# The wo products by one Strassen level, in a gated mix of windowed attention and a gMLP

## The chip, the cores and the metric

The kernel runs on 1 core of one Trainium2 chip. The metric is the device time of one execution in microseconds (us), the median of several runs; less is better. A core has TensorE (PE, matmuls into PSUM), VectorE (DVE), ScalarE (ACT), GpSimd (POOL) and SyncE (SP, which issues nearly all DMA here). Each engine takes its instructions in the order in which the program lists them.

## The reference

`x` is 2048 rows of 1024. All inputs are bfloat16.

```python
g = sigmoid((x * gate_w).sum(-1))
# A: 32 heads of 32, each position sees itself and 7 earlier ones, 2 apart
o = attention(x @ wqkv)                       # 2048 x 1024
a = o @ wo                                    # 1024 x 1024
# B: gMLP, half width 1792
z = gelu(x @ w_in); z1 = z[:, :1792]; z2 = layernorm(z[:, 1792:])
b = (z1 * (w_sp @ z2 + b_sp)) @ w_out         # w_sp is 2048 x 2048
out = g * a + (1 - g) * b
```

## The kernel before

One launch goes through stages that keep TensorE busy one after the other: the first z2 columns and the q, k, v projection of eight groups of four heads (L614), the rest of z2 (L319), z1 (L717), the mixer w_sp @ z2 (L732), the wo products (L890), and the gate stage, y @ w_out with the final sum (L732 again). The attention itself runs on VectorE, from the projection into the mixer, and writes o to DRAM in head order (`store_o`, L396).

The mixer and the gate stage already use one Strassen level (Winograd's form): a pair of row tiles of 128 is split in 2 x 2 blocks, and seven products take the place of eight. Operands are float16, scaled by powers of two that are read off the sum of absolute values, so that the sums of blocks do not overflow; an `Abs` activation with `accum_out` gives row sums, a matmul with a matrix of ones adds them over the partitions, and bit operations on the exponent make a power of two. In `g_group(n)` (mixer groups n = 0 to 15, each a pair of tiles and half of the columns) the products go to two PSUM banks `pa` and `pd` and a third bank `pb` that is forked off `pa` by ScalarE after the first product:

```python
product(pa, v.a11, b11, f0, f1, True)
pb = fork(pa, ZC, lo)
product(pd, v.s1, t1, f0, f1, True)
p5 = keep(pd, None)
product(pa, v.s2, t2, f0, f1, False)
u2 = keep(pa, lo)
```

So the third product waits for the fork (L756), the fifth for the snapshot `keep` (L742, L744), the seventh for the next one; `vec` (L748) adds on VectorE, L783 evicts the last product, L784 multiplies with z1. `y_norm` (L570) sums the absolute values of the group, `y_finish` scales it to float16 (L584) and `store_y` (L540) writes it to DRAM. For each pair the rows of w_sp are loaded transposed (`load_rows`, L485), scaled by VectorE (`scale_rows`, L492) and summed (`s_sums`, L496, L497).

The wo products take the o rows back transposed (`load_oT`, L455, 16 tiles of 128 rows into 16 places), with wo in the same order from DRAM (`load_wo`, L450), in bfloat16: 16 tiles x 2 halves of 512 columns x 8 matmuls. ScalarE evicts each half times the gate `g_s` into `mix` (L892). The gate stage adds `mix` at its end.

The order is by hand: `tc.manual_schedule()`, and a class `Beat` that counts the time TensorE ought to take (`BEAT`), and at the end of each product puts into the program what is due: steps given with `beat.at(time, fn)`. It decides order alone; when a step runs is up to the engines' queues. `w_out` is summed in eight pieces in the z1 stage (`load_w_piece` L547, `w_norm` L550), and loaded and scaled late (`load_w_out` L848 to L851, `w_scale` L856, `w_sums` L866, `y_sums` L870).

Of the kernel before, what the change touches and what calls it, by code (L numbers as in the profile page):

```python
# [10 lines left out]
F32 = mybir.dt.float32  # L11
# [4 lines left out]
P = 128  # L16
# [45 lines left out]
def kernel(  # L62
# [25 lines left out]
    def reg(off, n):  # L88
        return arena[:, off:off + n]
# [54 lines left out]
    yl = sm.tile([P, 32], F32, name="yl")  # L144
    ys = sm.tile([P, 16], F32, name="ys")
    wl = sm.tile([P, 8], F32, name="wl")
    wl_n = sm.tile([P, 1], BF, name="wl_n")
    wsc = sm.tile([P, 1], F32, name="wsc")
    rs_n = sm.tile([P, 16], BF, name="rs_n")
    cm05 = sm.tile([P, 16], F32, name="cm05")  # L150
    nc.gpsimd.memset(cm05[:], -0.5)
    att_L = sm.tile([P, 2 * W * 8 * HG], F32, name="att_L")
# [35 lines left out]
    class Pair:  # L188
        def __init__(self, off):
# [11 lines left out]
    snaps = [reg(o, 2 * ZC).bitcast(F32) for o in  # L201
             [X_OFF + 14336, X_OFF + 14336 + 896, SN_OFF, SN_OFF + 896, SN_OFF + 1792]]
    abs_waste = reg(SN_OFF + 2688, 896).rearrange("p (h f) -> p h f", h=2)
    rs_bc = [rs_b[:, 256 * r:256 * (r + 1)] for r in range(2)]

    y_ring = [reg(X_OFF + 7168 + r * 1792, 1792).bitcast(F16).rearrange("p (r h f) -> p r h f", r=2, h=2)
# [7 lines left out]
    e1, e2, e4 = [reg(F_OFF + 3584 * r, 3584).bitcast(F16).rearrange("p (k n) -> p k n", n=512) for r in range(3)]  # L214
    e3 = d12
    w_flat = B_w_out.rearrange("(p a) n -> p (a n)", p=P)
    w_pieces = [reg(T2_OFF + 3584 + 1792 * r, 1792) for r in range(2)]

    class Rows:
        def __init__(self, off):  # L220
# [7 lines left out]
    rows = [Rows(o) for o in (F_OFF + 10752, F_OFF + 17024, A_OFF, A_OFF + 6272, A_OFF + 12544)]  # L228
    keeps = [reg(S0_OFF + 1024 * r, 1024).bitcast(F32) for r in range(7)]
    mix = [reg(o, 2048).bitcast(F32) for o in [Z_OFF + 2048 * r for r in range(14)] + [T1_OFF, T1_OFF + 2048]]  # L230
    oT = [reg(o, 1024).rearrange("p (k t) -> p k t", k=KT)
          for o in [A_OFF + 1024 * r for r in range(11)] + [S0_OFF + 1024 * r for r in range(5)]]
    wo_sb = reg(A_OFF + 11264, KT * D).rearrange("p (k n) -> p k n", k=KT)
    ob_slots = [reg(o, 1024) for o in [F_OFF + 23296, F_OFF + 24320] + [Z_OFF + 2048 * r for r in range(14)]]

    x_v = x2.rearrange("(i q) d -> q i d", q=P)
# [188 lines left out]
    def attended():  # L425
        store_o(NG - 1)
        load_wo()
        prep["attended"] = True

    prep = {"at": 1e12, "normed": 0, "done": False, "attended": False, "o": 0}  # L430

    def vector_steps(t):
        for item in attention_steps(t):
# [13 lines left out]
                           A_wo.rearrange("(g h d) n -> h g d n", g=NG, h=HG, d=DH)[h])  # L447

    def load_wo():
        sync.dma_start(wo_sb, wop_d.rearrange("(k p) n -> p k n", p=P))  # L450

    def load_oT(limit):
        n = prep["o"]
        if n < limit:
            sync.dma_start_transpose(oT[n], o_d[n * P:(n + 1) * P, :])  # L455
            prep["o"] += 1

    def load_nat(a, slot):
        sync.dma_start(slot, wsp_v[a])
# [89 lines left out]
    def w_norm(m):  # L549
        nc.scalar.activation(w_pieces[m % 2], w_pieces[m % 2], ACT.Abs, accum_out=wl[:, m:m + 1])  # L550

    def w_total():
        nc.vector.memset(zeros[:], 1.0)
        nc.vector.tensor_reduce(wsc[:], wl[:], AX.X, ALU.add)
        nc.vector.tensor_copy(wl_n[:], wsc[:])

    def w_power():
        ps = psum.tile([P, 512], F32, name="ps", tag="ps")
        nc.tensor.matmul(ps[:, 0:1], ones, wl_n[:], start=True, stop=True)
        nc.vector.tensor_scalar(wsc[:], ps[:, 0:1], 2.0 ** -30, 2.0 ** -13, ALU.max, ALU.mult)  # L560
        nc.vector.tensor_scalar(wsc[:].bitcast(U32), wsc[:].bitcast(U32), EXPO, EXPO, ALU.bitwise_and, ALU.bitwise_xor)

    def load_rows_y(u):
        for r in range(2):
# [2 lines left out]
    def y_norm(n):  # L567
        for r in range(2):
            k = 2 * (2 * (n // 2) + r) + n % 2
            nc.scalar.activation(abs_waste, g_ring[n % 4][:, r], ACT.Abs, accum_out=yl[:, k:k + 1])  # L570

    def y_power(u):
        sl = slice(2 * u, 2 * u + 2)
# [125 lines left out]
    beat.at(t + 20.0, row_store)  # L699
    beat.at(t + 22.0, lambda: load_scale(0))  # L700
    for m in range(8):
        beat.at(t + 30.0 + 4.2 * m, lambda m=m: load_w_piece(m))
        beat.at(t + 36.5 + 4.2 * m, lambda m=m: w_norm(m))
    beat.at(t + 70.0, w_total)
    beat.at(t + 91.0, w_power)

    for c in range(4):
        w1 = w1_slots[c]
# [16 lines left out]
                                       ap=[[FH, P], [P * FH, 4], [1, ZC]]), z1s)  # L725
    assert prep["done"]
    beat.lead = MIX_LEAD

    def product(ps, w, v, c0, c1, first):
        K = v.shape[1]  # L730
# [82 lines left out]

    for n in range(2):
        load_z1(n)
    for n in range(2 * NU):
        u, fb = n // 2, n % 2
        t = beat.now
        if fb == 0 and u + 1 < NU:
            beat.at(t + 0.5, lambda u=u: load_scale(u + 1))  # L820
            for h in range(2):
                beat.at(t + 2.0, lambda u=u, h=h: load_rows(u + 1, h))
        g_group(n)
        if fb == 0 and u > 0:
            y_finish(u - 1)
        if fb == 0 and u + 1 < NU:
            for h in range(2):
                scale_rows(u + 1, h)
            beat.on_vector(2.5)
            for fn in s_sums(u + 1):  # L830
                fn()
            beat.on_vector(2.8)
        if prep["attended"]:
            limit = 16 if n >= 2 * NU - 3 else 11
            for m in range(6):
                beat.at(beat.now + 1.0 + 1.6 * m, lambda limit=limit: load_oT(limit))
    assert prep["attended"]

    t = beat.now
    beat.at(t + 5.0, lambda: y_norm(2 * NU - 1))  # L840
    beat.at(t + 7.0, lambda: y_finish(NU - 1))
    for m in range(16):
        beat.at(t + 1.0 + 1.6 * m, lambda: load_oT(16))

    def load_w_out(b):
        w = w_out_n[:, 7168 * b:7168 * (b + 1)].rearrange("p (k n) -> p k n", n=D)
# [6 lines left out]
    def w_scale(b):  # L853
        for m in range(4):
            sl = slice(7168 * b + 1792 * m, 7168 * b + 1792 * (m + 1))
            nc.vector.tensor_scalar(w_out_h[:, sl], w_out_n[:, sl], wsc[:], None, ALU.mult)  # L856

    def omegas():
        for x in (ys[:], wsc[:]):
            nc.vector.tensor_scalar(x.bitcast(U32), x.bitcast(U32), EXPO, EXPO, ALU.bitwise_and, ALU.bitwise_xor)  # L860
        nc.vector.scalar_tensor_tensor(omr[:], ys[:], 0.5, omr[:], ALU.mult, ALU.mult)
        nc.vector.tensor_scalar(omr[:], omr[:], wsc[:], 0.5, ALU.mult, ALU.mult)

    def w_sums():
        for out_, a, b in ((e1, d12, d11), (e2, d22, e1), (e3, d22, d12), (e4, d21, e2)):
            TT(out_, a, b, ALU.subtract)  # L866

    def y_sums(u):
        v = rows[u % 5]
# [2 lines left out]
        TT(v.s2, v.s1, v.a11, ALU.subtract)  # L872
        TT(v.s4, v.a12, v.s2, ALU.subtract)

    beat.at(t + 3.0, lambda: load_w_out(0))
    beat.at(t + 20.0, lambda: w_scale(0))
    beat.at(t + 30.0, lambda: w_scale(1))
    beat.at(t + 32.0, w_sums)
    beat.at(t + 36.0, omegas)
    for u in range(2):  # L880
        beat.at(t + 26.0 + 4.0 * u, lambda u=u: load_rows_y(u))
        beat.at(t + 44.0 + 4.0 * u, lambda u=u: y_sums(u))

    for a in range(16):
        if a == 12:
            beat.at(beat.now + 0.5, lambda: load_rows_y(2))
        for c in range(2):
            psa = bank()
            for kt in range(KT):
                nc.tensor.matmul(psa[:], oT[a][:, kt, :], wo_sb[:, kt, 512 * c:512 * (c + 1)],  # L890
                                 start=(kt == 0), stop=(kt == KT - 1))
            nc.scalar.activation(mix[a][:, 512 * c:512 * (c + 1)], psa[:], ACT.Copy, scale=g_s[:, a:a + 1])  # L892
            beat.run(KT * 512)
    beat.flush(1e9)

    kept = [0]
# [4 lines left out]
        nc.scalar.activation(out, ps[:], ACT.Copy, scale=scale)  # L901
        return out

    def finish(out, ps, scale, x):
        nc.vector.scalar_tensor_tensor(out, ps[:], scale, x, ALU.mult, ALU.add)  # L905

    for u in range(NU):
        v = rows[u % 5]
        lo, hi = [omr[:, 2 * u + h:2 * u + h + 1] for h in range(2)]
        m11, m12, m21, m22 = [mix[2 * u + h][:, 512 * c:512 * (c + 1)] for h in range(2) for c in range(2)]  # L910
        o11, o12, o21, o22 = [ob_slots[2 * u + h][:, 512 * c:512 * (c + 1)] for h in range(2) for c in range(2)]
        pa, pd = [psum.tile([P, 512], F32, name="ps", tag="ps") for _ in range(2)]
        if u == 0:
            for n in (3, 4):
                load_rows_y(n)
        product(pa, v.a11, d11, 0, 512, True)
        pb = fork(pa, 512, None)
        product(pd, v.s1, e1, 0, 512, True)
        p5 = hold(pd, hi)
        product(pa, v.s2, e2, 0, 512, False)  # L920
        u2 = hold(pa, lo)
        product(pb, v.a12, d21, 0, 512, False)
        finish(o11, pb, lo, m11)
        TT(u2, u2, m12, ALU.add)
        product(pa, v.s3, e3, 0, 512, False)
        u3 = hold(pa, hi)
        TT(p5, p5, m22, ALU.add)
        if 0 < u < NU - 1:
            y_sums(u + 1)
        product(pd, v.s4, d22, 0, 512, False)  # L930
        TT(o22, p5, u3, ALU.add)
        finish(o12, pd, lo, u2)
        sync.dma_start(out2[2 * u * P:(2 * u + 1) * P, :], ob_slots[2 * u])
        product(pa, v.a22, e4, 0, 512, False)
        finish(o21, pa, hi, m21)
        if u == NU - 1:
            sync.dma_start(out2[(2 * u + 1) * P:(2 * u + 2) * P, 512:D], o22)
            sync.dma_start(out2[(2 * u + 1) * P:(2 * u + 2) * P, 0:512], o21)
        else:
            sync.dma_start(out2[(2 * u + 1) * P:(2 * u + 2) * P, :], ob_slots[2 * u + 1])  # L940
        if u + 5 < NU:
            load_rows_y(u + 5)
# [30 lines left out]
```

## Time and profile before

| | us |
|---|---|
| median of 3 runs (lowest to highest) | 684.23 (683.94 to 684.54) |
| the profiled execution, its own time | 688.53 |
| its span, first to last instruction | 686.8 |
| z1 stage, start to end on TensorE | 270.6 to 369.8 |
| mixer | 369.8 to 543.3 |
| wo stage | 543.3 to 598.5 |
| gate stage | from 598.5 |

The mean granted clock is 0.998. Times in the text are counted from the start of the span. In lines of a timeline the first number is the start, the second the duration (of several instructions together where "x" is over 1), and a bracket is the idle time of the engine before it with what ended it. "SPq" lines are the issue of DMA, with the waiting of the queue.

### The profile page before, as it was taken

The numbers are of one execution on the slowest core, as the hardware profiler recorded it, in microseconds if no ns is written. First come the engines' busy times: TensorE is split into PE (matmuls) and PEld (weight loads), VectorE is DVE, ScalarE is ACT, GpSimd is POOL, SyncE is SP. The second block draws the span as 40 slices with busy tenths as digits, with TensorE's granted clock in tenths as the row PEclk, the third lists the DMA queues.
The fourth block names the chain that finished last, engine by engine and source line by source line (L and its number), as shares of the span: only waits on it lengthen the run. The fifth ranks groups of instructions, "written<-read, shape, count | busy, mean of one in ns | idle before, by whom it ended". The sixth has DMA issues, their size and how long they took to land.

```text
span 686.8 us, 9395 instructions
## 1 busy us (share of the span) xinstructions
PE 676.4 (98%) x3612; PEld 395.3 (58%) x3618; DVE 513.3 (75%) x554; ACT 366.8 (53%) x690; POOL 13.2 (2%) x23
## 2 busy tenths in 40 slices
PE   9999999999999999999899999999998999999997
PEld 4577788888875555555455555555554444444443
DVE  0009799999999999999999999999925356045645
ACT  4345666565545887848863464545544453422221
POOL 1000000000000000012100000000000000000000
PEclk9999999999999999999999999999999999999999
DMA  8999779999759751446845735595489997155211
GB/s 228 174 227 233 213 184 269 252 248 223 202 123 269 272 173 57 166 102 204 295 141 174 151 84 147 137 255 156 135 207 252 246 276 156 26 113 128 72 62 61
DMA packets 229148, 121.80 MB, mean 177 GB/s; under 512 B 190832, under 2 KB 215664, under 8 KB 229104
## 3 DMA queue, kind: packets, MB, share of 16 engines
q1 hardware_dynamic: 229104, 121.21, 67.1%
q8 instruction: 28, 0.46, 0.3%
q14 instruction: 16, 0.13, 0.1%
HBM read 61.87 MB, written 37.82 MB: 145 GB/s over the span
## 4 chain that ended last, share of the span: by engine, by line
PE 92%; DMA 3%; ACT 2%; SPq 2%; issue 0%; DVE 0%; ACTq 0%
PE ps L732 32%; PE ps L614 18%; PE ps L319 9%; PE ps L717 8%; PE sd L614 6%; PE ps L890 6%; PE seed L732 5%; PE sd L319 3%; PE sd L717 3%; PE sd L890 2%; SPq L599 1%; DMA z_d<-arena 1%; DMA arena<-in_A_wqkv_dram 1%; DMA y_d<-arena 1%; ACT arena L719 1%; ACT arena L550 1%
## 5 line engine op out<-in xcount | busy, mean ns | idle before, releaser
L732 PE MATMUL ps<-arena 128*128 128x448 f16 (+1 forms) x1104 | 223.9, 362 | 2.2 <-ACT arena L744 2.2
L732 PEld LDWEIGHTS <-arena 128*128 128x128 f16 x1288 | 126.5, 98 | 131.6 <-issue 4.5
L614 PEld LDWEIGHTS <-arena 128*128 128x128 bf16 x1024 | 141.6, 138 | 26.1 <-issue 1.4
L614 PE MATMUL ps<-arena 128*128 128x384 bf16 x768 | 130.3, 326 | 1.0 <-DMA arena<-in_A_wqkv_dram 1.0
L342 DVE TENSOR_TENSOR arena<-arena 128x8192 bf16<-128x8192 bf16 x16 | 70.8, 4422 | 47.3 <-DMA arena<-in_A_wqkv_dram 47.1
L345 DVE TENSOR_TENSOR arena<-arena 128x4096 bf16<-128x4096 bf16 (+1 forms) x64 | 77.6, 1212 | 2.0
L717 PEld LDWEIGHTS <-arena 128*128 128x128 bf16 x512 | 49.9, 98 | 48.5 <-issue 2.1
L717 PE MATMUL ps<-arena 128*128 128x448 bf16 x384 | 75.6, 352 | 1.8 <-ACT arena L719 1.8
L319 PE MATMUL ps<-arena 128*128 128x448 bf16 (+1 forms) x384 | 76.8, 353 | 0.5 <-DMA arena<-in_B_w_in_dram 0.5
L319 PEld LDWEIGHTS <-arena 128*128 128x128 bf16 x512 | 49.9, 98 | 47.1 <-ACT arena L306 0.7
L375 DVE TENSOR_TENSOR arena<-arena,att_A 128x8192 bf16<-128x8192 bf16 x16 | 70.7, 4421 | 0.2
L622 ACT CAST arena<-ps 128x384 bf16<-128x384 f32 x84 | 39.5, 484 | 45.0 <-PE ps L614 41.9
L905 DVE SCALAR_TENSOR_TENSOR arena<-seed,omr,arena 128x512 bf16<-128x512 f32 x8 | 6.0, 751 | 59.3 <-PE seed L732 59.3
L614 PE MATMUL sd<-arena 128*128 128x384 bf16 x256 | 46.8, 326 | 0.0
L890 PE MATMUL ps<-arena 128*128 128x512 bf16 x187 | 42.3, 379 | 0.2
L890 PEld LDWEIGHTS <-arena 128*128 128x128 bf16 x256 | 25.0, 98 | 30.2
L732 PE MATMUL seed<-arena 128*128 128x448 f16 (+1 forms) x184 | 40.2, 361 | 0.0
L325 ACT ACTIVATE arena<-ps 128x448 bf16<-128x448 f32 x48 | 26.1, 548 | 24.5 <-PE ps L319 23.9
L719 ACT ACTIVATE arena<-ps 128x448 bf16<-128x448 f32 x48 | 25.5, 570 | 25.4 <-PE ps L717 25.3
L381 DVE TENSOR_TENSOR arena<-arena 128x4096 bf16<-128x4096 bf16 x16 | 36.6, 2290 | 0.4
L744 ACT ACTIVATE arena<-ps,bt 128x448 f32<-128x448 f32 x32 | 20.3, 634 | 29.5 <-PE ps L732 29.4
L901 ACT ACTIVATE arena<-ps,omr 128x512 f32<-128x512 f32 x24 | 16.5, 688 | 32.7 <-PE ps L732 32.7
(121 smaller groups left out, 632.1 us busy)
## 6 DMA issues: line engine op xcount, KB each, us to landing
arena<-in_B_w_sp_dram SPq DMA_DIRECT2D x16, 512.0 KB, 5.2
arena<-k_d SPq DMA_DIRECT2D x8, 960.0 KB, 6.7
arena<-v_d SPq DMA_DIRECT2D x8, 960.0 KB, 6.0
z_d<-arena SPq DMA_DIRECT2D x16, 448.0 KB, 2.7
arena<-z_d SPq DMA_DIRECT2D x16, 448.0 KB, 3.6
y_d<-arena SPq DMA_DIRECT2D x16, 448.0 KB, 3.2
arena<-in_A_wqkv_dram SPq DMA_DIRECT2D x24, 256.0 KB, 5.4
arena<-in_B_w_in_dram SPq DMA_DIRECT2D x6, 896.0 KB, 8.0
```

The costliest lines, as they stand in the source:

```text
L319: nc.tensor.matmul(ps[:, 0:N], xT[:, kt, i * P:(i + 1) * P], w2[:, kt, ZC * c:ZC * c + N], start=(kt == 0), stop=(kt == KT - 1))
L325: nc.scalar.activation(z2[:, i, ZC * c:ZC * (c + 1)], ps[:, 0:ZC], ACT.Gelu_apprx_tanh, accum_out=s1[:, 4 * i + c:4 * i + c + 1])
L342: TT(prod.rearrange("p (w j c) -> p w j c", w=W, j=8, c=C), in0, in1, ALU.mult)
L345: return lambda: TT(pv[:, :, 0:half], pv[:, :, 0:half], pv[:, :, half:2 * half], ALU.add)
L375: TT(prod.rearrange("p (w j d h) -> p w j d h", w=W, j=8, d=DH, h=HG), in0, in1, ALU.mult)
L381: return [(4.4, mul), (2.3, lambda: TT(p3[:, 0:4, :], p3[:, 0:4, :], p3[:, 4:8, :], ALU.add)), (1.2, lambda: TT(p3[:, 0:2, :], p3[:, 0:2, ...
L614: nc.tensor.matmul(ps[:, 0:3 * C].rearrange("p (t c) -> p t c", t=3), lhsT, wgt[:, 0:3, kt, :], start=(kt == 0), stop=(kt == KT - 1))
L622: nc.scalar.copy(st[:, j % 4, :], ps[:, 0:3 * C])
L717: nc.tensor.matmul(ps[:, 0:ZC], xT[:, kt, i * P:(i + 1) * P], w1[:, kt, :], start=(kt == 0), stop=(kt == KT - 1))
L719: nc.scalar.activation(z1s[:, i % 4, :], ps[:, 0:ZC], ACT.Gelu_apprx_tanh)
L732: nc.tensor.matmul(ps[:, 0:c1 - c0], w[:, k, :], v[:, k, c0:c1], start=(first and k == 0), stop=(k == K - 1), skip_group_check=True)
L890: nc.tensor.matmul(psa[:], oT[a][:, kt, :], wo_sb[:, kt, 512 * c:512 * (c + 1)], start=(kt == 0), stop=(kt == KT - 1))
```

## The change

The wo stage takes one Strassen level: o's tiles are paired (`Heads`, 8 pairs u), o and wo are scaled to float16, and 7 products of 4 matmuls take the place of 8 per pair. Two pairs go side by side, product by product (`zip(wo_group(u), wo_group(u + 1))`). The scale of wo comes from its row sums in 11 pieces, taken on ScalarE in the mixer (`load_wo_chunk`, `wo_norm`); `w_total` and `w_power` now serve both weights and move from the z1 stage into the mixer. Each pair of o is normed on ScalarE (`heads_norm`), added up by a ones-matmul on TensorE between two VectorE steps (`heads_total`), scaled and summed on VectorE (`heads_sums`). The last steps of `wo_group` take the results out by ScalarE, or by VectorE's `finish`. wo sits at `A_OFF` now instead of `A_OFF + 11264`; the w_out pieces get other places and 5.2 instead of 4.2 between them; three matmuls into spare banks (`rest`) stand ahead of the mixer; the last of the w_out sums (e4) and `y_sums(1)` come after wo, and so do the loads of the y rows of pairs 2 to 4.

```diff
-    oT = [reg(o, 1024).rearrange("p (k t) -> p k t", k=KT)
-          for o in [A_OFF + 1024 * r for r in range(11)] + [S0_OFF + 1024 * r for r in range(5)]]
-    wo_sb = reg(A_OFF + 11264, KT * D).rearrange("p (k n) -> p k n", k=KT)
+    w_chunk = reg(SN_OFF + 3584, 768)
+    wo_n = reg(A_OFF, KT * D)
+    wo_h = wo_n.bitcast(F16)
...
 def attended():
         load_wo()
+        t = max(beat.now, beat.vector)
+        for u in range(2):
+            plan_heads(u, t + 5.0 + 7.0 * u)
+        for m in range(4):
+            beat.at(t + 11.0 + 1.5 * m, lambda m=m: wo_scale(m))
+            beat.at(t + 17.5 + 1.5 * m, lambda m=m: wo_sum(m))
+
+    def load_heads(u, r):
+        a = 2 * u + r
+        sync.dma_start_transpose(heads[u].raw[r], o_d[a * P:(a + 1) * P, :])
+
+    def plan_heads(u, t, late=0.0):
+        for r in range(2):
+            beat.at(t + 3.0 * r, lambda r=r: load_heads(u, r))
+        t = max(t, late - 9.0)
+        beat.at(t + 9.0, lambda: heads_norm(u))
+        beat.at(t + 13.0, lambda: heads_total(u))
+        beat.at(t + 15.0, lambda: heads_sums(u))
+
+    def heads_norm(u):
+        for r in range(2):
+            nc.scalar.activation(heads[u].waste, heads[u].flat[:, 1024 * r:1024 * (r + 1)], ACT.Abs,
+                                 accum_out=ol[:, 2 * u + r:2 * u + r + 1])
+
+    def heads_total(u):
+        TT(ol_n[:, u:u + 1], ol[:, 2 * u:2 * u + 1], ol[:, 2 * u + 1:2 * u + 2], ALU.add)
+        ps = psum.tile([P, 512], F32, name="ps", tag="ps")
+        nc.tensor.matmul(ps[:, 0:1], ones, ol_n[:, u:u + 1], start=True, stop=True)
+        nc.vector.tensor_scalar(osc[:, u:u + 1], ps[:, 0:1], 2.0 ** -30, 2.0 ** -13, ALU.max, ALU.mult)
...
+    def heads_sums(u):
+        v = heads[u]
+        nc.vector.tensor_scalar(v.half, v.flat, osc[:, u:u + 1], None, ALU.mult)
+        TT(v.s1, v.a21, v.a22, ALU.add)
+        TT(v.s3, v.a11, v.a21, ALU.subtract)
+        TT(v.s2, v.s1, v.a11, ALU.subtract)
+        TT(v.s4, v.a12, v.s2, ALU.subtract)
...
+    def load_wo_chunk(m):
+        n = min(768, 8192 - 768 * m)
+        sync.dma_start(w_chunk[:, 0:n], wo_flat[:, 768 * m:768 * m + n])
+
+    def wo_norm(m):
+        n = min(768, 8192 - 768 * m)
+        nc.scalar.activation(w_chunk[:, 0:n], w_chunk[:, 0:n], ACT.Abs, accum_out=s2[:, m:m + 1])
...
-        beat.at(t + 30.0 + 4.2 * m, lambda m=m: load_w_piece(m))
-        beat.at(t + 36.5 + 4.2 * m, lambda m=m: w_norm(m))
-    beat.at(t + 70.0, w_total)
-    beat.at(t + 91.0, w_power)
+        beat.at(t + 30.0 + 5.2 * m, lambda m=m: load_w_piece(m))
+        beat.at(t + 37.0 + 5.2 * m, lambda m=m: w_norm(m))
...
+    rest = [seeded.tile([P, 512], F32, name="rest", tag="sd") for _ in range(2)]
+    for r in (0, 1, 0):
+        nc.tensor.matmul(rest[r][:], ident[:], mask[:], start=True, stop=True)
...
     for n in range(2):
         load_z1(n)
+    for m in range(11):
+        beat.at(beat.now + 3.0 + 8.0 * m, lambda m=m: load_wo_chunk(m))
+        beat.at(beat.now + 9.0 + 8.0 * m, lambda m=m: wo_norm(m))
+    beat.at(beat.now + 96.0, w_total)
+    beat.at(beat.now + 104.0, w_power)
...
+        if n == 2 * NU - 3:
+            plan_heads(2, beat.now + 1.0)
+            plan_heads(3, beat.now + 7.0, beat.now + 2 * 7 * KT * ZC * BEAT + 0.5)
...
+    for m in range(4, 7):
+        plan_heads(m, t + 0.5 + 5.0 * (m - 4))
...
-    for a in range(16):
-        if a == 12:
-            beat.at(beat.now + 0.5, lambda: load_rows_y(2))
-        for c in range(2):
-            psa = bank()
-            for kt in range(KT):
-                nc.tensor.matmul(psa[:], oT[a][:, kt, :], wo_sb[:, kt, 512 * c:512 * (c + 1)],
-                                 start=(kt == 0), stop=(kt == KT - 1))
-            nc.scalar.activation(mix[a][:, 512 * c:512 * (c + 1)], psa[:], ACT.Copy, scale=g_s[:, a:a + 1])
-            beat.run(KT * 512)
+    def wo_group(u):
...
+        product(pa, v.a11, c11, 0, 512, True)
+        pb = fork(pa, 512, None)
+        yield
+        product(pd, v.s1, h1, 0, 512, True)
+        p5 = wo_hold(pd, hi)
+        yield
+        product(pa, v.s2, h2, 0, 512, False)
+        u2 = wo_hold(pa, lo)
+        yield
+        product(pb, v.a12, c21, 0, 512, False)
+        nc.scalar.activation(m11, pb[:], ACT.Copy, scale=lo)
+        yield
+        product(pa, v.s3, h3, 0, 512, False)
+        finish(m22, pa, hi, p5)
+        yield
+        product(pd, v.s4, c22, 0, 512, False)
+        finish(m12, pd, lo, u2)
+        yield
+        product(pa, v.a22, h4, 0, 512, False)
+        nc.scalar.activation(m21, pa[:], ACT.Copy, scale=hi)
+        yield
+
+    for u in range(0, NU, 2):
+        while prep["heads"] < u + 2:
+            assert beat.later
+            beat.flush(beat.later[0][0])
+        for _ in zip(wo_group(u), wo_group(u + 1)):
+            pass
+        if u == 0:
+            plan_heads(7, beat.now + 0.5)
+    w_sums(3)
+    y_sums(1)
```

## The prediction

> **What bounds the kernel now.** I read the page first, then TensorE's waits, the chain of waits, the timelines of ScalarE, VectorE and the SP queue around the mixer, and a table of ten-microsecond windows.
>
> ```profile
> PE   676.4 (98%) x3612; PEld 395.3 (58%) x3618; DVE 513.3 (75%) x554; ACT 366.8 (53%) x690; POOL 13.2 (2%) x23
> ...
> PE 92%; DMA 3%; ACT 2%; SPq 2%; issue 0%; DVE 0%; ACTq 0%
> ```
> ```profile
> PE ps L732 <- ACT arena L744: 2.2, 1, 2.2
> PE ps L717 <- ACT arena L719: 1.8, 1, 1.8
> ```
> ```profile
> 530.00:540.00 10.00, 10.00 (x46) 4.78 (x44) 3.68 (x10) 4.36 (x9) 0.00 (x0) 0.83 1.09 223
> ```
> TensorE is the bound: 98% busy, 92% of the chain, and only two waits of size. So a product less is time gained, and any wait of TensorE is time lost. The window (its last three columns are granted clock, DMA share and GB/s) shows the price of a wait: after TensorE stood idle for 2.16 us up to 529.49, the clock over the next ten microseconds was 0.83, that is 3.4 us at half speed, another 1.7 us lost. The 1.8 us wait at 340.7 left no such mark.
>
> ```profile
> 591.79 5.18 PE ps L890 x24
> ...
> 668.19 9.06 PE ps L732 x42
> ```
> In the chain of waits 24 wo products of 512 columns take 5.18 us, 0.216 us each, and float16 ones 9.06/42 = 0.216: the type costs nothing.
>
> **The change, part by part.** *Products.* 256 wo matmuls become 8 pairs x 7 x 4 = 224. 32 x 0.216 = 6.9 us less; the stage of 55.3 us (543.28 to 598.53) would take 48.4. All else the change does is put into queues that run in order, so each item counts where it waits.
>
> *The first wo piece, in the mixer.* `wo_norm(0)` stands on ScalarE between the third snapshot of mixer group 0 and that group's last eviction (L783 before); the fork of group 1 (L756) comes after. Its transfer stands on SP behind the two transposes of the next w_sp rows.
>
> ```profile
> 376.76 6.83 SPq L485 DMA_TRANSPOSE arena<-in_B_w_sp_dram  x2
> 388.90 0.37 SPq L534 DMA_DIRECT2D arena<-z_d  x1
> ```
> ```profile
> 380.57 0.64 ACT L783 ACTIVATE arena<-ps,bt 128x448 bf16<-128x448 f32 x1 [2.39 <-PE ps L732]
> 382.15 0.61 ACT L756 ACTIVATE seed<-ps,bt 128x448 f32<-128x448 f32 x1 [0.94 <-PE ps L732]
> ```
> SP is held by VectorE (the o store waits for L378 until 370.2), then by z stores, z1 loads and those transposes until 376.76 + 6.83 = 383.6; nothing in the change moves that. The 192 KB piece lands 2.5 to 3.5 us after its issue (2.5 is the median of 128 KB q_d stores, 3.5 of one 448 KB z1 load): 386.1 to 387.1, I take 386.7. The norm of 768 columns takes 0.96 with its read-out (two of 896 start 1.07 apart), L783's and L756's successors 0.53 + 0.61: the fork is there at 388.8. TensorE's third product of group 1, which needs it, started at 369.8 + 10.59 + 3.03 = 383.4. So the mixer is 5.4 us later from there on. This is an absolute time, so neither the 1.8 us wait before the mixer (the wider spacing of the w_out norms puts the exponential's table reload ahead of the late piece, and ScalarE evicts at about 338 instead of 341.9: gone) nor the three `rest` matmuls (0.65 us plus 0.6 of waiting for the last z1 eviction) add to the sum. TensorE stands some 5.9 us, and a clock loss as after 529 follows: 1.7 (0.9 to 2.6, by where the slow stretch falls). Together **+7.1**. The other ten pieces: each load waits for the norm before it, and on my walk down SP's order all land in time but number 8, behind the next transposes, about at the limit: 0.2 at most 1.
>
> [...]
>
> *The end of the mixer.* There VectorE has waited for TensorE (0.85 us before L784 at 476.6), so VectorE and SP are late by as much as TensorE, and I use before's times and compare inside them.
>
> ```profile
> 496.94 0.57 SPq L396 DMA_DIRECT2D o_d<-arena  x1
> 502.96 0.37 SPq L450 DMA_DIRECT2D arena<-wop_d  x1
> 503.43 10.41 SPq L485 DMA_TRANSPOSE arena<-in_B_w_sp_dram  x2
> ```
> ```profile
> 514.35 1.23 DVE L492 TENSOR_TENSOR arena<-arena,rs_b 128x2048 f16<-128x2048 bf16 x1 [4.90 <-DMA arena<-in_B_w_sp_dram]
> 516.54 1.22 DVE L492 TENSOR_TENSOR arena<-arena,rs_b 128x2048 f16<-128x2048 bf16 x1 [0.96 <-DMA arena<-in_B_w_sp_dram]
> ...
> 520.94 1.54 DVE L584 TENSOR_SCALAR arena<-arena,ys 128x896 f16<-128x896 bf16 x4
> ```
> The last w_sp rows land only at 514 and 516.5. wo now loads into a place that o's store does not read, so it no longer waits 5.4 us for it; but it queues behind the same bytes, and I give the rows 2.5 us (0 to 6): 511.8 and 514.0. Behind them come the transposes of the first two tiles of o. Each took 4.7 to 5.2 us to land; from 512.1 the second lands at 518.2. ScalarE has `heads_norm(0)` ahead of the snapshot that group 13's last product needs: two of 1.17 from 516.8, ending 519.4, then 0.63. TensorE wants it at 507.6 + 9.08 = 516.7 and gets it at 520.1. Then, at the border to group 14 (518.2 undisturbed), TensorE has the ones-matmul of `heads_total(0)`. VectorE reaches its operand after the second row scaling by 5.9 us (as now, 516.54 to 522.4), four wo scalings (2048 columns, 0.70 each by 2.47 for four of 1792), two L748 (0.53), one wo sum (1.13, by 7.95 for four of 3584) and the total (0.2): 514.0 + 5.9 + 5.2 = 525.1. So group 14 starts 7.0 late, whatever the first wait was. Clock 1.7 more. In group 15 two norms and two y norms (4.5 us) hold the fork 0.55 too long, and `heads_total(2)`, behind `y_scale(6)`, comes 1.2 late. Sum 10.5 to 10.8, against the 4.0 that this stretch loses now (mixer of 16 x 10.59 = 169.5, measured 173.5): **+6.8** (+3 to +10). The present wait (y stores behind four o transposes) has only two ahead of it and goes.
>
> *The wo stage.* Times from its start, undisturbed pair of groups 12.1. First pair: forks wait for `heads_norm(3)` (0.4), the last of the y norms holds a snapshot (0.95): 13.6. Second pair: VectorE has `heads_sums(5)` (0.70 + 4 x 0.35 + 0.5 = 2.6) before a `finish` (0.75): 0.9 late, 26.7. Then TensorE meets `heads_total(6)`; VectorE has still to do two finishes, four w_out scalings (2.5) and another finish, and comes at 30.1: 3.4. One step on, `heads_total(7)` stands behind `heads_sums(6)`: 1.5. Clock 1.7. Third and fourth pair then run free (second half of w_out scaled at 39, wanted at 44). 48.4 + 0.4 + 0.95 + 0.9 + 3.4 + 1.5 + 1.7 = 57.3 and rounding in the walk 0.5: 57.8 against 55.3, **+2.5** (-4 to +6). Undone products are thus more than eaten. The o transposes of tiles 12 to 15 now come after the second w_out load; they land at 23 to 26, just before ScalarE takes them.
>
> *Gate stage.* e4, y_sums(1) and three row loads move behind wo. e4 takes 2.0 and is wanted 9.1 us in; the rows are wanted by L870 18 us in, two transposes (4.5 us each at most) after wo's end: hidden. Nothing added.
>
> **Sum.** 0.2 + 7.1 + 6.8 + 2.5 = +16.6. The profiled execution took 688.53 us (span 686.8), the median of the runs is 684.23; I take the shift as the same: 705.1 profiled, **700.8**.
>
> **Rivals.** *Faster.* The totals' waits vanish: the last w_sp rows land by 507, eight to ten microseconds sooner, because o's store and wo run side by side. Then group 14 waits for nothing, VectorE enters wo some 7 us ahead and reaches `heads_total(6)` in time. Left are +7.1, +0.2, -4.0 and -6.9: 680.6. For it: DMA share is only 0.50 and 0.73 at 490 to 510. Against: rows behind 2 MB took 10.4 us of SP, behind nothing 5.5 to 7. It decides below 507. 8%.
> *Half of it.* One stage keeps its waits, the other not: 700.8 less 6.8 or less 9 (57.8 to 48.8): about 693. 17%.
> *Later still.* SP's blocking y store and second w_out load push tiles 12 to 15 beyond 26 us in the wo stage; each microsecond counts, since ScalarE holds the evictions behind both norms and TensorE both totals; with the 7.4 us that a w_out load took here, +7: 707.8. 11%.
> *Nothing at all*, within 0.2% of before (about what a measurement of this kernel can tell from no change): losses of 6.9 net of the 4.0 that goes, 2%.
>
> **Numbers.** Forecast 62%. The range leaves out the fast rival, a part of the late one, and takes in the half one and the bounds of the three sums: 689 to 708. Faster 0.09 (the rival and a little more), same 0.02, slower 0.89.
>
> **What would show it.** In the profile after: a ScalarE wait for the A_wo transfer before its first norm, and a TensorE wait of 5 to 6 us on ScalarE near 383; a granted clock under 1 in that window, near 520 and in the wo stage; TensorE waits on VectorE at the ones-matmuls; wo stage over 55 us with 224 matmuls. Wrong if TensorE's waits sum to under 5 us, or if the piece lands before 381.

## The result

The changed kernel takes 702.25 us, the median of 4 runs (701.77 to 703.92), beside 684.26 us of the kernel before: a ratio of 1.0267, 95% interval 1.025 to 1.0285, 18.0 us slower. The forecast was 700.8, the range 689 to 708. Sign, place and most of the mechanism came out as forecast; the closeness of the number is luck, as two errors of opposite sign nearly cancel: a loss of some 4 us taken off twice, and a wo stage forecast 3.0 us too long. Both are worked out below.

The page of the changed kernel, busy time of the engines and shares of the chain that ended last:

```profile
PE 675.5 (96%) x3596; PEld 393.9 (56%) x3597; DVE 555.6 (79%) x660; ACT 395.5 (56%) x752; POOL 13.1 (2%) x23
...
PE 89%; DVE 3%; DMA 2%; ACT 2%; SPq 2%; issue 1%; DVEq 0%; ACTq 0%
```

TensorE is busy 675.5 us as against 676.4 although it has 32 matmuls less in the wo stage: part of its work now runs at a low clock (0.990 granted on average, 0.998 before). Of the span it is idle 24.5 us (700.0 less 675.5), where it was 10.4. VectorE, absent from the chain before, now holds 3% of it. TensorE's waits (line, what it waited for and who had to write it, us in total, times, longest):

```profile
PE ps L485 <- DVE rs_n L483: 8.3, 4, 3.0
PE ps L823 <- ACT seed L847: 6.0, 2, 5.3
PE ps L823 <- ACT arena L835: 3.4, 1, 3.4
...
PE ps L823 <- DVE arena L980: 0.7, 1, 0.7
...
PE ps L823 <- ACT arena L990: 0.3, 1, 0.3
```

The ones-matmuls of the totals (L485) wait for VectorE; products (L823) wait for ScalarE's fork (L847) and for its third snapshot (L835). The waits for totals and fork are new; for the third snapshot (L744 before) TensorE waited 2.2 us in the profile of before too. The windows of ten microseconds in which the loss lies (columns: length, busy time of PE, PEld, DVE, ACT and POOL with counts, then granted clock, DMA share, GB/s):

```profile
380.00:390.00 10.00, 4.72 (x21) 2.08 (x19) 9.52 (x9) 2.42 (x5) 0.00 (x0) 0.80 0.75 136
390.00:400.00 10.00, 10.00 (x47) 4.93 (x46) 6.01 (x9) 5.54 (x11) 0.00 (x0) 0.86 0.49 123
520.00:530.00 10.00, 6.50 (x33) 3.08 (x32) 9.06 (x17) 6.04 (x12) 0.00 (x0) 0.96 1.16 240
530.00:540.00 10.00, 7.11 (x31) 3.33 (x31) 9.61 (x18) 4.31 (x8) 0.00 (x0) 0.69 0.87 238
580.00:590.00 10.00, 5.11 (x25) 2.01 (x23) 9.16 (x26) 5.46 (x10) 0.00 (x0) 1.00 1.10 209
```

TensorE works for less than half of 380 to 390, and its clock stays low into the next window. From 520 to 540 it works for two thirds of the time, and the clock is low behind the waits. At 580 to 590 it stands nearly as long as in the first window, at full clock.

By stage, from the first matmul of one to the first of the next in the timeline of TensorE (a second profile of the kernel before was taken for the first experiment):

```
                   before, as    before,    forecast   after
                   shown above   again
mixer starts at      369.8        369.7      369.8     369.1
mixer                173.5        169.5      187.6     187.9
wo stage              55.3         55.3       57.8      54.8
gate stage            88.3         88.2       88.3      88.2
span                 686.8        682.6      703.5     700.0
```

An undisturbed mixer takes 169.5, so the changed one loses 18.4. The wo stage with its 224 matmuls should take 48.4 and takes 54.8. Nearly all of the 6.9 us of saved matmuls is thus spent on 6.4 us of new loss in their own stage, and the mixer's loss is the whole slowdown.

**Near 383.** ScalarE and the SP queue of the changed kernel:

```profile
376.36 6.96 SPq L563 DMA_TRANSPOSE arena<-in_B_w_sp_dram  x2
383.36 4.12 SPq L632 DMA_DIRECT2D arena<-in_A_wo_dram  x2
```
```profile
376.88 0.63 ACT L835 ACTIVATE arena<-ps,bt 128x448 f32<-128x448 f32 x1 [0.98 <-PE ps L823]
386.18 0.84 ACT L636 ACTIVATE arena<-arena 128x768 bf16<-128x768 bf16 x1 [8.66 <-DMA arena<-in_A_wo_dram]
...
387.02 0.61 ACT L874 ACTIVATE arena<-ps,bt 128x448 bf16<-128x448 f32 x1
387.54 0.60 ACT L847 ACTIVATE seed<-ps,bt 128x448 f32<-128x448 f32 x1
```

SP is through with the two transposes at 383.32 and issues the wo piece; the norm (L636) gets it at 386.18 after 8.66 us of standing; the last eviction of group 0 (L874) and the fork of group 1 (L847) come right behind. Forecast were issue at 383.6, landing at 386.7, fork by 388.8; it was done at 388.1.

**The end of the mixer.** What held group 13 and then the ones-matmul at its border:

```profile
505.44 2.49 SPq L534 DMA_DIRECT2D arena<-wop_d  x1
508.02 11.94 SPq L563 DMA_TRANSPOSE arena<-in_B_w_sp_dram  x2
...
520.68 2.94 SPq L467 DMA_TRANSPOSE arena<-o_d  x2
```
```profile
525.06 1.06 ACT L479 ACTIVATE arena<-arena 128x1024 bf16<-128x1024 bf16 x1 [2.91 <-DMA arena<-o_d]
```
```profile
527.97 1.90 PE L823 MATMUL ps<-arena 128*128 128x448 f16 x8 [3.36 <-ACT arena L835]
532.89 0.16 PE L485 MATMUL ps<-rs_n,zeros 128*128 128x1 bf16 x1 [3.04 <-DVE rs_n L483]
```
```profile
520.07 1.23 DVE L570 TENSOR_TENSOR arena<-arena,rs_b 128x2048 f16<-128x2048 bf16 x1 [2.74 <-DMA arena<-in_B_w_sp_dram]
```

wo's 2 MB (L534) are issued first, the w_sp rows take 11.94 us of SP behind them, the first o tiles follow at 520.7 and land at 525. TensorE waits 3.36 us for the snapshot that stands behind their norm. It waits another 3.04 us for the total, which stands on VectorE behind the scaling of the late rows (L570) and all that follows it.

### The profile page after: what moved, and what is told of

The parts are those of the page before. It is cut to its first block, busy times and chain, and to the rows that moved or that the text cites. A ratio compares the mean times of both kernels' runs of the same rounds, so it can differ in the third digit from the quotient of the medians.

```text
span 700.0 us, 9585 instructions
## 1 busy us (share of the span) xinstructions
PE 675.5 (96%) x3596; PEld 393.9 (56%) x3597; DVE 555.6 (79%) x660; ACT 395.5 (56%) x752; POOL 13.1 (2%) x23
## 4 chain that ended last, share of the span: by engine, by line
PE 89%; DVE 3%; DMA 2%; ACT 2%; SPq 2%; issue 1%; DVEq 0%; ACTq 0%
PE ps L823 33%; PE ps L704 18%; PE ps L805 10%; PE ps L348 9%; PE sd L704 6%; PE seed L823 6%; PE sd L805 3%; PE sd L348 3%; SPq L689 1%; DMA arena<-in_A_wo_dram 1%; DMA arena<-in_A_wqkv_dram 1%; DMA arena<-in_B_w_sp_dram 1%; ACT arena L479 1%; SPq L687 0%; ACT arena L660 0%
## 5 line engine op out<-in xcount | busy, mean ns | idle before, releaser
L823 PE MATMUL ps<-arena 128*128 128x448 f16 (+1 forms) x1296 | 268.9, 366 | 10.4 <-ACT seed L847 6.0
L823 PEld LDWEIGHTS <-arena 128*128 128x128 f16 x1512 | 148.3, 98 | 175.2 <-issue 24.6
L704 PEld LDWEIGHTS <-arena 128*128 128x128 bf16 x1024 | 141.6, 138 | 25.6 <-issue 0.9
L348 PEld LDWEIGHTS <-arena 128*128 128x128 bf16 x512 | 50.2, 98 | 46.9 <-issue 0.7
L805 PEld LDWEIGHTS <-arena 128*128 128x128 bf16 x512 | 50.0, 98 | 46.6
L823 PE MATMUL seed<-arena 128*128 128x448 f16 (+1 forms) x216 | 48.6, 368 | 0.0
L835 ACT ACTIVATE arena<-ps,bt 128x448 f32<-128x448 f32 x32 | 20.2, 633 | 25.9 <-PE ps L823 23.1
L540 ACT ACTIVATE arena<-arena 128x2048 bf16<-128x2048 bf16 x16 | 30.8, 1926 | 0.3 <-DMA arena<-in_B_w_sp_dram 0.3
L660 ACT ACTIVATE arena<-arena 128x896 bf16<-128x896 bf16 x32 | 30.3, 946 | 0.5
```

The costliest lines, as they stand in the source:

```text
L348: nc.tensor.matmul(ps[:, 0:N], xT[:, kt, i * P:(i + 1) * P], w2[:, kt, ZC * c:ZC * c + N], start=(kt == 0), stop=(kt == KT - 1))
L540: nc.scalar.activation(waste, slot, ACT.Abs, accum_out=l1[:, a:a + 1])
L660: nc.scalar.activation(waste, g_ring[n % 4][:, r], ACT.Abs, accum_out=yl[:, k:k + 1])
L704: nc.tensor.matmul(ps[:, 0:3 * C].rearrange("p (t c) -> p t c", t=3), lhsT, wgt[:, 0:3, kt, :], start=(kt == 0), stop=(kt == KT - 1))
L805: nc.tensor.matmul(ps[:, 0:ZC], xT[:, kt, i * P:(i + 1) * P], w1[:, kt, :], start=(kt == 0), stop=(kt == KT - 1))
L823: nc.tensor.matmul(ps[:, 0:c1 - c0], w[:, k, :], v[:, k, c0:c1], start=(first and k == 0), stop=(k == K - 1), skip_group_check=True)
```

## The experiments

The kernel before took 684.27 to 684.83 us beside these runs and 684.26 beside the changed kernel's 702.25, so gains counted from 702.25 are good to about 0.6 us.

**Is the profile of before a normal run?** It took 688.53 us where the timed runs took 684.2. The kernel before was profiled once more, unchanged.

> The kernel before, unchanged, profiled once more. Theory (the profile of before was a normal run, only taken under a longer one): span 686 to 687, TensorE waits of 1.8 us at L717 and 2.2 us at L732 again, clock 0.83 in a ten-microsecond window near 530. Rival (the profiled execution of before was an unlucky one, and the 684.2 us of the timed runs lacks some of these waits): span near 682.5, with one of the two waits gone or without a slow clock behind it, so that the change added some 4 us more than a comparison of the two profiles says.

```profile
PE ps L717 <- ACT arena L719: 1.8, 1, 1.8
```
```profile
530.00:540.00 10.00, 10.00 (x54) 5.09 (x52) 3.71 (x10) 5.55 (x10) 0.00 (x0) 1.00 1.02 240
```

Span 682.6, time 684.39. The wait of 1.8 us in the z1 stage is there, the wait of 2.2 us for L744 and the clock of 0.83 are not: TensorE is busy for the whole of every window from 500 to 560 at clock 1.00. The rival is right. The wait behind the y stores belongs to some executions of the kernel before only, the mixer of its ordinary run loses nothing, and 4.0 of the 4.3 us between the profiled and the timed runs lie there (mixer 173.5 against 169.5). Why one execution has it and another not, no run shows.

**The wo pieces in the mixer.** First all eleven were moved 14 us; then they were given 10 us each, with 9 us between load and norm.

```
- load_wo_chunk(m) at +3.0 + 8.0 m,  wo_norm(m) at +9.0 + 8.0 m
+ first run:   +17.0 + 8.0 m  and  +23.0 + 8.0 m    (w_total, w_power 14 later)
+ second run:  +15.0 + 10.0 m and  +24.0 + 10.0 m   (w_total, w_power 30 later)
```

> The changed kernel with the eleven wo pieces, their norms and their total 14 us later, so that the first piece is queued behind the third z1 load and its norm stands behind the fork of mixer group 2. Theory (queue order: the norm waits for a transfer that SP issues behind two transposes): the 5.3 us wait near 383, the 0.7 us wait near 454 and the slow clock behind the first (two stretches of 3.4 us, 4.4 us of matmuls in them at half speed, 2.2 us) are gone, 702.3 - 5.3 - 2.2 = 694.8 with 694 to 696 taken as agreement; the waits at the end of the mixer stay, as VectorE and SP there are late by as much as TensorE. Rival (the pieces cost by what they move or by ScalarE's 11 x 1.0 us, not by their place): the waits only move to another piece, 699 or more.

> The changed kernel with the wo pieces alone rearranged: every 10 us, each load planned 9 us ahead of its norm, the first 12 us later (in the first such run one piece was still issued 4 us ahead of its norm, and TensorE stood 1.9 us for it). Theory: none of the eleven norms holds TensorE, the first term of the sum goes as a whole: 5.3 + 0.7 of waiting and 2.2 of slow clock, 702.3 - 8.2 = 694.1, 693 to 695. Rival (a norm always meets some late piece, the DMA engines being half busy all through the mixer): a wait on ScalarE of 1 us or more stays between 370 and 500, 696 or more.

The first took 696.62 us (694.63 to 697.1), 5.6 less than the changed kernel. The waits at 383 and 454 and the slow clock behind the first are gone, and another piece is late now, a snapshot behind its norm holding TensorE:

```profile
443.43 6.21 PE L823 MATMUL ps<-arena 128*128 128x448 f16 x32 [1.89 <-ACT arena L835]
```

That piece was issued at 437.3, just ahead of two row transposes, and its norm began at 441.9. Theory and rival each have a part. The second run took 693.03 us (692.64 to 694.95), 9.2 less, with no wait of TensorE from 370 to 500, as the theory said. By the start of mixer group 13 it is 8.0 us ahead of the changed kernel (507.38, not 515.36). The rest comes at the end of the mixer, where the total waits 1.87 us instead of 3.04 and the clock is slow for 3.4 us instead of 6.8. What costs is the place of a piece among SP's transfers and the distance to its norm; with both right, all eleven norms fit in without holding TensorE.

**The end of the mixer.** The 2 MB of wo were first put behind the last w_sp rows alone, then behind the first four o tiles too, with wo's scalings and sums behind the totals and sums of those tiles.

```
  in attended():      - load_wo()
  in the group loop:  + if u + 2 == NU: beat.at(t + 2.0, load_wo)       # behind load_rows(7)
  second run, ahead of it:  + load_heads(a // 2, a % 2) for a in 0..3
                      wo_scale(m) at t + 27.6 + m (was 11.0 + 1.5 m), wo_sum(m) at t + 31.6 + m (was 17.5 + 1.5 m)
```

> The changed kernel with one edit at the end of the mixer: the 2 MB load of wo is queued behind the last two w_sp row transposes, not ahead of them. Theory (the rows are late because they queue behind wo, and all VectorE work up to the first ones-matmul is late with them): the rows land some 7 us sooner, the o tiles too, the waits of 3.4 us (third snapshot of group 13) and 3.0 us (ones-matmul of the first pair of o tiles) and the 1.6 us of slow clock go: 702.3 - 8 = 694.3, 693 to 696. Rival (wo then lands later by as much, and its four scalings, which stand on VectorE ahead of the total, wait for it instead): the wait of 3.4 goes and that of 3.0 stays or grows, 699 to 702.

> The changed kernel with the end of the mixer queued anew: the last two w_sp rows, then the first four tiles of o, then the 2 MB load of wo, and wo's four scalings and sums on VectorE behind the totals and sums of the first two pairs of tiles. Theory (after the run with rows ahead of wo: whatever is queued behind wo's 2 MB lands some 8 us late, and that is where the waits at groups 13 and 14 come from): the o tiles land near 517 and not 525, the waits of 3.4 us and 3.0 us and the 1.6 us of slow clock go, 702.3 - 8 = 694.3, 692.5 to 696. Rival (VectorE is simply full there, some 30 us of work from the landing of the rows to the wo stage): the waits come back at the start of the wo stage, where its second product needs wo's first sum, 698 or more.

The first brought 700.44 us (699.61 to 702.25), 1.8 less. Its range overlaps that of the changed kernel, so the reading rests on the waits. In its SP queue and on ScalarE:

```profile
504.53 7.40 SPq L562 DMA_TRANSPOSE arena<-in_B_w_sp_dram  x2
511.98 0.57 SPq L533 DMA_DIRECT2D arena<-wop_d  x1
...
513.28 9.53 SPq L466 DMA_TRANSPOSE arena<-o_d  x2
```
```profile
524.17 1.06 ACT L478 ACTIVATE arena<-arena 128x1024 bf16<-128x1024 bf16 x1 [2.97 <-DMA arena<-o_d]
```

The rows need 7.40 us of SP and not 11.94, and VectorE scales them at 516.3 without waiting, not at 520.1. But the o tiles now queue right behind wo, and their norm starts at 524.17, hardly sooner than 525.06. The wait for the snapshot stayed (3.41 us), the one for the total shrank to 0.93. Part of that gain does not show in the time, as in this run's profile the clock drops behind the seventh pair's total (0.66 from 580 to 590; 1.00 in the changed kernel). It is the reverse of the rival and half of the theory: two waits with two causes, the rows for the total, the o tiles for the snapshot; both causes are wo's bytes ahead of them.

With o tiles ahead of wo as well: 697.58 us (696.47 to 699.36), 4.7 less. Both waits are gone (0.34 us left of the first). In their place the total of the third pair of o tiles, just ahead of group 15's fourth product, waits (lines of the edited kernels are off by a few: L484 here is L485):

```profile
545.95 0.16 PE L484 MATMUL ps<-rs_n,zeros 128*128 128x1 bf16 x1 [3.76 <-DVE rs_n L482]
```

So the rival is half right too: a loss comes back one total later, 3.76 us instead of 1.08, behind the four scalings and the first sum of wo. But VectorE is not simply full. Before that it stands 3.25 us for a z1 tile, whose load is queued right behind wo's 2 MB:

```profile
530.62 1.09 DVE L874 TENSOR_TENSOR arena<-arena 128x1792 bf16<-128x1792 bf16 x1 [3.25 <-DMA arena<-z_d]
```

How the 3.76 us divide between this and the steps on wo, this run does not show.

**The wo stage.** The first half of w_out is scaled 5 us earlier; then also its second half is loaded later.

```
- beat.at(t + 22.0, lambda: w_scale(0))
+ beat.at(t + 17.0, lambda: w_scale(0))
  second run also: load_w_out(1) at max(beat.now, beat.vector) + 8.0 (was 0.6)
```

> The changed kernel with the four scalings of the first half of w_out planned 5 us sooner, so that they stand ahead of the total of the sixth pair of o tiles and no longer ahead of the seventh pair's. Theory of the prediction (the seventh pair's total is late because of those scalings): its wait of 2.75 us goes to 0.3 or less and the next one (1.46) shrinks, 702.3 - 2.5 to 4 = 698.3 to 699.8. Rival (the total waits for the norm of a tile that lands at 583.3, behind the second load of w_out on SP): ScalarE ends that norm at 584.6, so the wait shrinks by 0.9 alone, 701.4, 701 to 702.

> The same, and the second load of w_out queued behind the last three transposes of o tiles. Theory (scalings and landing together hold the two totals): both waits (2.75 and 1.46) go, 702.3 - 4 = 698.3, 697.5 to 699.3. Rival (VectorE is full from the third pair to the end of the wo stage, so that what it does not do late for a total it does late for the gate stage): the gate stage starts as late as before, 701 to 702.5.

698.77 us (697.66 to 699.32) and 699.51 us (697.83 to 699.73). TensorE at the seventh and eighth pair's ones-matmul, the first of the two kernels:

```profile
583.23 0.16 PE L485 MATMUL ps<-rs_n,zeros 128*128 128x1 bf16 x1 [0.36 <-DVE rs_n L483]
...
586.60 0.16 PE L485 MATMUL ps<-rs_n,zeros 128*128 128x1 bf16 x1 [1.46 <-DVE rs_n L483]
```

The 2.75 us became 0.36. In the changed kernel VectorE is busy up to that total, with the scalings among its work, so they held it, as the prediction had it. The tile that the rival names landed sooner in this run (its norm began at 581.52, not 583.33, in a stage that began 0.7 earlier), so the rival's bound of 0.9 did not bind; why it landed sooner is not shown, so it is not shown either that moving the scalings alone would gain more than 0.9. The stage shortens by 2.0 us (52.8 after 54.8), as a new wait of 0.42 came at the sixth pair's total; the rest of the 3.5 between the medians lies elsewhere. Loading w_out later still made no further difference. The 1.46 us stayed in both; they are the sums of the seventh pair (L493 to L500, 2.6 us), which stand on VectorE ahead of the eighth pair's total, as the prediction also had it.

**What the new work on VectorE costs by itself.** The norms and the totals of o were left out, with a constant scale for o; wo's scale is still worked out, from what `s2` held before.

```
- load_wo_chunk / wo_norm, heads_norm, heads_total
+ nc.vector.memset(osc[:, u:u + 1], 1.0)      # in heads_sums
```

> The changed kernel with the norms of wo and of o and the totals of o left out (constant scales instead: the scaling, the sums, the 224 products and the transfers of o and of wo itself stay; the wo pieces are not loaded). Theory (the loss is all in waits for norms and totals): 684.3 - 6.9 = 677.4 less what the mixer end of before loses by its y stores (up to 4), so 673 to 678. Rival (the scalings and sums on VectorE, 13 more microseconds of scaling and sums beside the last two mixer groups and 8 x 2.6 in all, or the transposes, cost by themselves): 682 or more.

679.62 us (678.41 to 680.16), ratio to before 0.9931 (0.9917 to 0.9946): 4.6 us faster, not the 6.3 or more of the theory, and not the rival's 682. The span is 676.6 against 682.6 of the second profile of before. The mixer loses nothing; the wo stage takes 50.6 and not 48.4, of which 1.6 us are two waits for a `finish` behind other VectorE work. No run here got more out of the 32 matmuls.

**The spacing of the w_out norms alone**, in the kernel before (pieces at T4_OFF, 5.2 us apart).

> The kernel before with only the wider spacing of the w_out norms (5.2 us, pieces in the other place). Theory: the one wait of the z1 stage goes (1.8 us on ScalarE near 342), nothing else: 684.3 - 1.8 = 682.5, 682.0 to 683.0. Rival (the time comes back in the mixer, whose start is an absolute time set by SP's queue): no difference, 684.0 to 684.6.

684.13 us (12 runs) beside 684.80 (23 runs) of the kernel before, ratio 0.9985 (0.9974 to 0.9997). The wait of 1.8 us is gone, two of 0.66 and 0.17 us for VectorE came in mixer group 2: some of it is given back, and what is left is between both expectations.

**All of it mended.** One kernel with the second version of each; one with the total of the third pair 5.5 us later and a z1 load ahead of wo; one with that total 4 us later again, behind the first 12 matmuls of the wo stage.

```
  heads_total(u) at t + 13.0, heads_sums(u) at t + 15.0 become
+ second:  total {2: 18.5, 6: 13.6, 7: 15.8}, sums {2: 19.5, 7: 17.0}; load_wo at t + 9.0
+ third:   total {2: 22.5, 3: 15.0, 6: 13.6, 7: 15.8}, sums {2: 23.5, 3: 16.0, 7: 17.0}
```

> All three mended: wo pieces every 10 us, each load 9 us ahead of its norm, the first 12 us later; o tiles ahead of wo at the end of the mixer; w_out's first half scaled early and its second half loaded late. Theory (the change loses by queue places alone, in three separate stretches): 702.3 - 8.2 - 8 - 4 = 682.1, 680 to 685, which is faster than the kernel before (684.3). Rival (one stretch only hands its loss on to the next, VectorE being full from the end of the mixer on): 688 or more.

> All three mended as before, and what was left there: the total and sums of the third pair of o tiles 5.5 and 4.5 us later (TensorE stood 3.5 us for it in group 15, and ran 1.7 us slow behind that), those of the seventh and eighth pair 0.6 to 2.8 us later (1.5), and a z1 load ahead of wo's 2 MB. Theory: 688.4 - 3.5 - 1.7 - 1.5 = 681.7, 680 to 683.5; then the 32 products saved are worth most of their 6.9 us. Rival (VectorE is full from group 13 to the end of the wo stage and only passes the wait on): the second product of the wo stage or a finish waits instead, 685 or more.

> As the last kernel, with the total and sums of the third pair of o tiles planned 4 us later again, which puts its ones-matmul behind the first 12 products of the wo stage, and those of the fourth pair 1 to 2 us later. Theory (the place of a ones-matmul on TensorE is what costs; VectorE has the total ready at 541.4, TensorE now comes to it near 546): the wait of 3.3 us and the 1.6 us of slow clock behind it go, 685.8 - 4.9 = 680.9, 680 to 683, faster than before. Rival (VectorE is full, it only passes the wait on, to a finish or to the second pair): 684 or more.

```
            this kernel, us (range)     before    ratio to before (95%)
first       688.41 (687.84 to 689.27)   684.63    1.0032 (0.9986 to 1.0079)
second      685.79 (684.47 to 690.49)   684.80    1.0016 (0.9997 to 1.0034)
third       683.73 (682.91 to 685.36)   684.83    0.9979 (0.9961 to 0.9997)
```

The first two came out where their rivals said (688 or more, 685 or more). One by one the three mends brought 9.2, 4.7 and 2.7 us, 16.6 together; in one kernel they bring 13.8, so the gains do not add up. TensorE at that total in the second kernel, VectorE at the total of the second pair there, and the largest waits of the third:

```profile
541.63 0.16 PE L484 MATMUL ps<-rs_n,zeros 128*128 128x1 bf16 x1 [3.27 <-DVE rs_n L482]
```
```profile
526.24 0.16 DVE L485 TENSOR_SCALAR var<-ps 128x1 f32<-128x1 f32 x1 [3.04 <-PE ps L484]
```
```profile
PE ps L822 <- DVE arena L983: 2.8, 4, 1.7
PE ps L484 <- DVE rs_n L482: 1.7, 3, 0.9
```

Moving the total by 5.5 us changed its wait from 3.54 to 3.27 us only: TensorE came to it later, and VectorE, with the four wo sums now all ahead of it, was ready later. The z1 load ahead of wo brought nothing either: VectorE no longer stood for the tile, but then stood 3.04 us for the second pair's ones-matmul, which TensorE does at its own place in the order. Another 4 us took the wait to 0.90 and the slow clock away (1.000 over the run), but put 1.69 us on a `finish`: between theory (680 to 683) and rival (684 or more). In the end the change, with every queue place mended, gains 1.1 us, 0.2%, at an interval that just leaves out no change. The spacing of the w_out norms, which is in all these kernels, brought 0.15% alone. So whether Strassen in the wo stage adds anything to that, these runs do not show.

## Why the prediction was right, and where it was not

*The products*: 6.9 us were forecast. With norms and totals away the change as a whole brings 4.6, of which about 1 us is the spacing of the w_out norms.

*The first wo piece* (+7.1): right in mechanism and size. Wait 5.28 us (5.9 forecast), the slow clock 6.83 us long and not 3.4 (0.80 and 0.86 of two windows are 4.0 and 2.8 us at half speed), in which 4.57 us of matmuls cost 2.3 (1.7 forecast). The piece behind the later transposes cost 0.67 (0.2, at most 1). Mending the pieces brought 9.2 us, somewhat more than these 8.2.

*The end of the mixer* (+6.8): right in its waits. The rows were scaled from 520.07 and 521.99 on, which less the 7.9 us by which the changed kernel is late there is 512.2 and 514.1 (511.8 and 514.0 forecast). The snapshot's wait was 3.36 (3.4 forecast), group 14 started 7.0 late as in the walk (at 532.92, where group 13's start of 515.36 plus 10.59 would have had it at 525.95), the slow clock behind that cost 1.6 (1.7), the third pair's total 1.08 (1.2); only the late fork of group 15 (0.55) did not come. That is 9.7 for 10.5 to 10.8, or 5.7 for 6.8 after the 4.0 that the profile of before loses there and the changed kernel does not.

*The step from profile to median* is one that failed: "I take the shift as the same". The sum of 705.1 was already rid of the wait behind the y stores (the 4.0 taken off at the end of the mixer); that wait was also 4.0 of the 4.3 us by which the profile of before lay above the median, as its second profile shows. Taking 4.3 off once more counted it twice. The sum itself should have stood as the forecast of the median; the changed kernel's profile (701.77) and median (702.25) are alike.

*The wo stage* (+2.5) is the other, a term that was mis-sized: the stage took 54.8, not 57.8, 0.5 less than before. These 3.0 us are most of what 705.1 is too high by. The snapshot behind the norms held TensorE 0.33 us (0.4 and 0.95 forecast), a finish 0.69 (0.9), the seventh pair's total 2.75 (3.4), the eighth's 1.46 (1.5); a slow clock of 1.7 us did not come. With the 48.4 these waits make 53.6; the remaining 1.1 is not taken apart (the run without norms and totals has 0.6 of it left as well). Forecast too high were the clock by 1.7, the y norms by 1.0, the totals and the finish by 0.9 and the rounding by 0.5; the remainder was not forecast. The length of the wait does not tell why the clock did not drop: behind the same 2.74 or 2.75 us it fell to 0.83, 0.66 and 0.83 (means of ten microseconds) in three of the edited kernels and stayed at 1.00 in a fourth (last section). "Over 55 us" and "clock under 1 in the wo stage" were the two signs that failed.

*Gate stage*: 0 forecast, 0 found.

*Rivals.* The fast one needed the rows before 507: SP was busy with them until 519.96, which is 512.1 in the times of before. "Half of it" needed one of the two stages free of waits, and both had them. For "later still" the last tile that counted came 26.3 us into the wo stage (583.33), at the edge of its condition, but VectorE's total was later than the tile.

## What to carry to other kernels

Cost every added load and reduction at the place in its queue where it stands: here a norm of 1.0 us (0.84 and 0.19 to read its sum out), for whose transfer ScalarE stood 8.66 us, held the eviction and the fork behind it, and TensorE for 5.28 us. Put a transfer that the next work needs ahead of a large one (the w_sp rows took 7.40 us of SP ahead of wo's 2 MB and 11.94 behind it), and move a total's matmul to where its operand is surely ready (its wait went from 3.27 to 0.90 us). Before taking a wait of one profile as a property of the kernel, compare the profiled time with the median: of the 4.3 us between them here, 4.0 were a wait and its slow clock that the second profile did not have.

## What the hardware showed that I had not expected

The length of a wait did not decide in these runs whether the clock dropped behind it. At the seventh pair's total the changed kernel stood 2.75 us and went on at full clock (1.00 from 580 to 600), and so did the run with the wo pieces 10 us apart (2.75 us, 1.00 from 570 to 590). In the run with the pieces 14 us later the same wait, 2.74 us, was followed by 0.83:

```profile
580.00:590.00 10.00, 8.82 (x36) 3.62 (x36) 9.13 (x26) 6.80 (x12) 0.00 (x0) 0.83 0.74 145
```

It was also followed by a slow clock with the rows ahead of wo (2.74 us, 0.66 from 580 to 590) and with the o tiles ahead of wo (2.75 us, 0.83 there). In that last run the wait of 3.76 us left no trace (clock 1.00 from 540 to 560), while the 2.16 us of before did (0.83 from 530 to 540).

The trace of the changed kernel also holds when the granted clock changed. Its two slow stretches in the mixer were at half clock (0.50) and 6.83 us long; from the second to 600 the clock was full (1.00), through the waits of 2.75 and 1.46 us (columns as above):

```profile
385.92:392.75 6.83, 4.57 (x13) 1.90 (x13) 6.34 (x7) 3.05 (x6) 0.00 (x0) 0.50 0.33 96
529.28:536.11 6.83, 3.79 (x12) 1.48 (x11) 6.54 (x11) 1.26 (x4) 0.00 (x0) 0.50 0.82 222
536.11:600.00 63.89, 57.59 (x282) 26.77 (x281) 47.74 (x120) 45.62 (x82) 0.00 (x0) 1.00 0.68 163
```

What else decides whether the clock drops, these runs do not show. The prediction charged 1.7 us at each of three places, an estimate from the one slow clock of before; found were 2.3 us behind the first wo piece, 1.6 at the end of the mixer and none in the wo stage.
